# Position bias of an attention layer: coefficients in two fp16 parts under a scale found on the chip, and bias columns in another order

## The chip, the cores and the metric

The kernel runs on one core of a Trainium2 chip. The metric is the device time of one execution in microseconds (us). Five engines work side by side, each through its own instructions in a fixed order: PE (TensorE, matmuls; its weight loads are shown as PEld), DVE (VectorE), ACT (ScalarE), POOL (GpSimd) and SP (SyncE, which issues most DMAs). An instruction that waits holds up everything behind it on its engine, and nothing on the others unless they need its result.

## The reference

The program is an attention layer with a bias that depends on position, and behind it a gated feed-forward layer over all 2304 tokens:

```
q, k, v: (4, 8, 576, 64);  w1: (1, 32), b1: (32,), w2: (32, 8)
scores  = q @ k^T / sqrt(64)
x       = log1p(|i - j|) / log1p(max(i, 1))          # one number for each pair of positions
bias    = relu(x * w1 + b1) @ w2                     # (576, 576, 8), the same for all batches
attn    = softmax(scores + bias) ;  out = attn @ v
y       = (sigmoid(out @ w_gate) * (out @ w_val)) @ w_out
```

Inside the relu, each of the 32 hidden units is either off or a straight line in x. So for a given pair (i, j) the bias of head h is `A * x + B`, where A is the sum of `w2 * w1`, and B the sum of `w2 * b1`, over the units that are on. The kernel computes it so.

## The kernel before

`tile_kernel` first calls `bias`, then runs `attention` (units of one batch and two heads), then `Moe.run` (the feed-forward layer). The order of the instructions on every engine is written out in the Python code (`manual_schedule`), and so fixed.

**The bias stage.** The 576 columns j are worked off in nine chunks of 64 (`for c in range(NCH)`). For a chunk, 16 "indicator" tiles say which hidden unit is on: a tile has 4 columns j times 32 units on its partitions and all 576 rows i along it. Twelve of the 16 (`OWN`) are made by two matmuls into a PSUM tile `y` (L405) and a Sigmoid on ACT (L410); the first chunk makes some on DVE (L408). The other four (`DPAIRS`, tile `far`) are made by DVE from tables (`apart`, L423). The tiles of chunk c+1 are made while chunk c is summed: the lists `YPOS` and `DPOS` say behind which sums each is made.

The sums are matmuls with an indicator as stationary operand and the coefficients `cfs` as moving operand (`sums`, L429): 64 columns wide (A and B, 8 heads, 4 columns j). The coefficients `cf` are fp32. They are split into three bf16 parts (L472, L474), and each sum is three matmuls, one for each part. A chunk has five blocks of rows in the order `BORD` (blocks 0, 1, 4, 2, 3): four with 128 rows and 16 sums each, and block 4 with the last 64 rows and 8 sums. Every block has a PSUM tile `bps`, of which there are two. When its sums are done, `leave` takes it off: DVE multiplies the A half by x (`btmp`, L437, or L450 for block 4), and then the B half is added: by DVE straight from PSUM (L445, two instructions of 384 and 128 elements), or, for block 0 (`BPOOL`) and block 4, by ACT copying B into `brest` (L440) and POOL adding (L445, L455).

Beside this, in the order of each engine: `conv` lets DVE and ACT narrow weights for the feed-forward layer, a step behind each block (L227 on ACT, L230 to L239 on DVE), from 512 KB loads `cvw`; in chunks 3 to 6 a matrix of v is loaded as `vb` and multiplied with itself (`gram`, L352); in chunk 7 a power of two as scale for v is found (`fit`, L366 to L380). The last chunk makes no indicators. In front of the first chunk, 12 matmuls on zeros (L290) run while the small inputs arrive.

**The feed-forward stage.** `Moe.run` works through `ORDER` ("A0 A1 B0 A2 B1 A3 ..."): a step takes one of two token blocks (A, B) through one of 12 weight blocks. Each step has 12 matmuls into `pg`, 12 into `pu` (L999), and 9 into `po` for the step before (L1023). Weights are narrowed and split as they are needed: `convert` begins one new block and moves each block under way on by one step (size on ACT L227; clamp on DVE L230; bit operations on DVE L233, L236, L239; upper part on ACT L953; lower part on DVE L962). `pg` and `pu` have one buffer each. The three strings of `START` are done before the loop, in step 0 and in step 1; "s" issues a load, "w5" moves weight block 5 on by a step.

## Time and profile before

| | us |
|---|---|
| median of 3 runs (768.4 to 769.64) | 768.56 |
| the profiled execution, its own time | 767.42 |
| its span, first to last instruction | 765.6 |
| bias stage: first sum to first score matmul after the last chunk | 14.07 to 112.84 |
| feed-forward stage begins (first matmul of L999) | 343.9 |
| busy over the span: PE, DVE, ACT, POOL | 725.9, 625.8, 546.7, 335.4 |
| mean granted TensorE clock | 0.994 |

The profiled execution took 1.8 us more than its span, and 1.1 us less than the median. How to read what is shown below: a line of the timeline has start, duration, engine, source line, operation and operands, "x18" for so many instructions merged, and in brackets the idle time ahead of it with what ended it. A line of windows has a stretch, its length, the busy time (and number of instructions) of PE, PEld, DVE, ACT and POOL in it, the granted TensorE clock (1.00 is 2.4 GHz, 0.50 is 1.2 GHz), the busy share of the DMA engines and GB/s.

### The profile page before, as it was taken

To read this page: it belongs to the slowest core of one execution; us is meant where nothing else is said; L and a number is where in the kernel's file an instruction comes from. 1 tells how busy PE (TensorE), PEld (TensorE's weight loads), DVE (VectorE), ACT (ScalarE), POOL (GpSimd) and SP (SyncE) were. 2 spreads that over 40 slices of the span, in tenths; PEclk is the share of its full clock that TensorE was granted. 3 is DMA by queue.
4 is the path that set the end of the run, shared out by engine and by line. 5 is a ranking of instruction groups with operands and counts; after the bars stand their busy time and mean duration, and the time that the engine had idled before them with its cause. 6 is when DMAs were issued, how large, how long until landed. Compare 5 with 4: busy or idle time off the path is not lost.

```text
span 765.6 us, 17842 instructions
## 1 busy us (share of the span) xinstructions
PE 725.9 (95%) x6705; PEld 532.7 (70%) x6705; DVE 625.8 (82%) x1333; ACT 546.7 (71%) x1187; POOL 335.4 (44%) x430
## 2 busy tenths in 40 slices
PE   7998978999999998989999999989999999999997
PEld 4888866777777776768998999845555555555553
...
GB/s 208 134 200 190 148 61 113 176 177 192 152 203 166 172 216 216 174 199 323 190 251 249 183 100 96 128 192 151 81 83 83 56 56 131 145 48 64 56 1 82
DMA packets 128598, 111.85 MB, mean 146 GB/s; under 512 B 78848, under 2 KB 99456, under 8 KB 128512
## 3 DMA queue, kind: packets, MB, share of 16 engines
...
## 4 chain that ended last, share of the span: by engine, by line
PE 62%; DVE 9%; ACT 8%; DMA 3%; issue 3%; ACTq 0%; SPq 0%; POOL 0%; DVEq 0%
PE po L1023 17%; PE pg L1171 11%; PE pu L1171 8%; PE pg L999 6%; PE pu L999 6%; PE acc L743 5%; PE sc L635 4%; DVE en L651 4%; PE pt L680 3%; ACT at L565 3%; DVE at L566 3%; ACT en L656 2%; PE sc L624 1%; DMA vr<-in_v_dram 1%; DMA wo<-scratch 1%
## 5 line engine op out<-in xcount | busy, mean ns | idle before, releaser
L1129 POOL TENSOR_TENSOR ws<-wm 128x256 f32<-128x256 f32 x44 | 40.7, 924 | 284.9 <-ACT wv L1135 143.4
L1171 PEld LDWEIGHTS <-wv 128*128 128x128 f16 x1008 | 98.0, 98 | 84.0 <-issue 9.0
L656 ACT ACTIVATE en<-en,mn 128x576 f32<-128x576 f32 x144 | 110.7, 773 | 16.9 <-DVE mn L651 16.7
L1171 PE MATMUL pg<-xq,wv 128*128 128x384 f16 x576 | 109.3, 326 | 2.6 <-ACT c L1197 2.2
L651 DVE CUSTOM_DVE_ANT_0 en<-sc,bias 128x576 f32<-128x576 f32 x128 | 91.7, 754 | 10.1 <-PE sc L635 9.3
L674 POOL TENSOR_TENSOR cr<-en,cr 128x512 f16<-128x512 f32 x124 | 89.4, 742 | 5.2
L1023 PE MATMUL po<-wo,gh 128*128 128x512 f16 x288 | 85.7, 379 | 0.0
L1171 PE MATMUL pu<-xq,wv 128*128 128x384 f16 x432 | 82.0, 326 | 1.9 <-DVE c L1177 1.9
L635 PE MATMUL sc<-k,part 64*128 64x288 f32 x768 | 75.0, 314 | 3.5 <-DVE bias L445 1.8
L566 DVE SCALAR_TENSOR_TENSOR at<-pt,at 128x512 f16<-128x512 f32 (+3 forms) x132 | 72.0, 565 | 7.3 <-ACT at L565 5.8
L1177 DVE TENSOR_TENSOR c<-pu,c 128x384 f32<-128x384 f32 x72 | 39.9, 555 | 43.5 <-PE pu L1171 28.5
L635 PEld LDWEIGHTS sc<-k,part 64*128 64x128 f32 x768 | 58.7, 187 | 19.0 <-issue 10.8
L429 PE MATMUL bps<-cfs,ind 128*128 128x64 bf16 x1458 | 67.5, 193 | 3.5 <-DVE bias L445 1.7
L410 ACT ACTIVATE ind<-y 128x576 bf16<-128x576 f32 x100 | 62.4, 651 | 10.8 <-PE y L405 8.0
L743 PE MATMUL acc<-at,vv 128*64 128x288 f16 x868 | 65.8, 289 | 3.1 <-ACT xe L747 1.1
L565 ACT ACTIVATE at<-pt 128x512 f16<-128x512 f32 (+3 forms) x132 | 61.6, 493 | 8.9 <-PE pt L680 7.6
L429 PEld LDWEIGHTS <-ind 128*128 128x128 bf16 x1458 | 58.7, 98 | 9.7 <-issue 3.1
L1189 ACT ACTIVATE gh<-c 128x384 f16<-128x384 f32 x48 | 25.1, 522 | 54.7 <-DVE c L1187 53.3
L680 PE MATMUL pt<-ident,en 128*128 128x128 f32 x328 | 53.0, 285 | 7.8 <-ACT en L656 5.1
L743 PEld LDWEIGHTS <-vv 128*64 128x64 f16 x896 | 48.1, 109 | 17.7 <-issue 15.1
L1023 PE MATMUL po<-wo,gl 128*128 128x512 f16 x144 | 54.6, 379 | 0.0
L999 PE MATMUL pg<-xhi,w 128*128 128x384 f32 x192 | 53.8, 339 | 0.2
...
## 6 DMA issues: line engine op xcount, KB each, us to landing
...
```

The costliest lines, as they stand in the source:

```text
L429: nc.tensor.matmul(out=o, lhsT=st, rhs=cfs[:, part], start=(part == 0), stop=(part == 2))
L565: nc.scalar.activation(out=hi, in_=ps, func=AF.Copy, scale=float(2.0 ** up))
L566: return lambda: nc.vector.scalar_tensor_tensor(out=lo, in0=ps, scalar=float(2.0 ** up), in1=hi, op0=ALU.mult, op1=ALU.subtract)
L635: nc.tensor.matmul(out=pair[h][:, e, 0:HF], lhsT=qs[rows, l, 128 * it:128 * it + 128], rhs=ks[rows, r, HF * e:HF * e + HF], start=(i == 0) ...
L651: nc.vector.tensor_tensor_reduce(out=half(en), in0=ps[:, :, 0:HF], in1=half(nbias), scale=-0.125, scalar=3.0e38, op0=ALU.add, op1=ALU.min, ...
L656: nc.scalar.activation(out=en, in_=en, func=AF.Exp, bias=mn, scale=-1.0, accum_out=sm)
L674: nc.gpsimd.tensor_tensor(out=t[:, a:a + z.stop - z.start], in0=en[:, z], in1=t[:, z], op=ALU.subtract)
L680: nc.tensor.transpose(pt[:, J], en[:, 128 * J:128 * J + 128], ident)
L743: nc.tensor.matmul(out=acc[D * h:D * h + D, 0:HF], lhsT=vv[:, h, J, z], rhs=at[:, h, y, cs], start=(i == 0), stop=(i == len(mms) - 1))
L999: self.nc.tensor.matmul(out=(pg, pu)[z], lhsT=l, rhs=r, start=(kc == 0 and i == 0), stop=(kc == 3 and i == 2))
L1023: self.nc.tensor.matmul(out=po, lhsT=l[:, tt], rhs=r, start=(first and i == 0), stop=(last and i == 2))
L1171: nc.tensor.matmul(out=p, lhsT=W[i][:, l, at + kc], rhs=V[b][:, r, kc], start=(new and n == 0), stop=(n == 5), skip_group_check=not new)
```

## The change

1. The coefficients are split into two fp16 parts instead of three bf16 parts, and `sums` issues two matmuls instead of three. For this they are multiplied by a power of two `cup`, and the result is multiplied by `cun`. Both are found on the chip: ACT sums the squares of `cf`, POOL rounds the sum, a matmul with ones adds it over the partitions, and six small DVE instructions (`scales`) make the two powers of two.
2. The A half is unscaled by multiplying the table `xt` by `cun` once (five POOL instructions). The B half is unscaled where it is added: DVE's addition becomes a `scalar_tensor_tensor` with `cun` as a per-partition scalar, and ACT's copy takes `cun` as its scale.
3. The bias columns are stored in another order (first the first 32 columns of every chunk, then the second 32), so that the written pieces of a head are one run. The keys and values are put into the same order on the host.
4. In `START`, "w5 w5" moves from step 0 to step 1.

```diff
-START = 'w2 w3 w3 w2 w4 s w4 s', 's s s s w5 w5', ''
+START = 'w2 w3 w3 w2 w4 s w4 s', 's s s s', 'w5 w5'
...
+    order = np.arange(S).reshape(NCH, 2, 32).transpose(1, 0, 2).reshape(S)
+    data["k"], data["v"] = np.ascontiguousarray(data["k"][..., order]), data["v"][:, :, order]
...
-        biasL = keep.tile([128, NP, S], F32, name="biasL")
+        biasL = keep.tile([128, NP, 2, HF], F32, name="biasL")
...
+        nc.scalar.activation(out=room, in_=cf.rearrange("p a h g -> p (a h g)"), func=AF.Square, accum_out=total)
+        nc.gpsimd.tensor_copy(out=cmost, in_=total)
+        nc.tensor.matmul(out=ps[:, 0, 0:1], lhsT=ones, rhs=cmost, start=True, stop=True)
...
+            m, up, un = (t.bitcast(I32) for t in (total, cup, cun))
+            e = nc.vector
+            e.tensor_scalar(out=total, in0=ps[:, 0, 0:1], scalar1=float(2.0 ** -80), scalar2=None, op0=ALU.max)
+            e.tensor_scalar(out=m, in0=m, scalar1=1, scalar2=None, op0=ALU.logical_shift_right)
+            e.tensor_scalar(out=up, in0=m, scalar1=0x1FC00000 - (11 << 23), scalar2=None, op0=ALU.add)
+            e.tensor_scalar(out=un, in0=m, scalar1=0x1FC00000 - (12 << 23), scalar2=None, op0=ALU.add)
+            e.tensor_scalar(out=up, in0=up, scalar1=0x7F800000, scalar2=0x7F800000, op0=ALU.bitwise_and, op1=ALU.bitwise_xor)
+            e.tensor_scalar(out=un, in0=un, scalar1=0x7F800000, scalar2=None, op0=ALU.bitwise_and)
+        scales()
+        for n in range(5):
+            w = S if n < 4 else S - 32
+            nc.gpsimd.tensor_scalar(out=xt[:, n, 0:w], in0=xt[:, n, 0:w], scalar1=cun, scalar2=1.0, op0=ALU.mult, op1=ALU.mult)
...
-            for part in range(3):
-                nc.tensor.matmul(out=o, lhsT=st, rhs=cfs[:, part], start=(part == 0), stop=(part == 2))
+            for part in range(2):
+                nc.tensor.matmul(out=o, lhsT=st, rhs=cfs[:, part], start=(part == 0), stop=(part == 1))
...
-                nc.scalar.activation(out=rest, in_=ps[:, 0:n, 1], func=AF.Copy)
+                nc.scalar.activation(out=rest, in_=ps[:, 0:n, 1], func=AF.Copy, scale=cun)
...
-                rest, add = ps[:, 0:n, 1], nc.vector
+                rest = ps[:, 0:n, 1]
+                def put(out, in0, in1):
+                    nc.vector.scalar_tensor_tensor(out=out, in0=in0, scalar=cun, in1=in1, op0=ALU.mult, op1=ALU.add)
...
-                if not sub:
-                    nc.vector.tensor_copy(out=cfs[:, part], in_=cf)
-                elif part < 2:
-                    nc.vector.tensor_tensor(out=cf, in0=cf, in1=cfs[:, part], op=ALU.subtract)
+            if i == CFI:
+                nc.vector.tensor_scalar(out=cfs[:, 0], in0=cf, scalar1=cup, scalar2=None, op0=ALU.mult)
+                nc.vector.scalar_tensor_tensor(out=cfs[:, 1], in0=cf, scalar=cup, in1=cfs[:, 0], op0=ALU.mult, op1=ALU.subtract)
```

Three places show what moves. The first is DVE in front of the first chunk, before the change; `dist` and `edge` are the tables for `far`, and `ind` the indicators that DVE makes itself:

```order
L331 TENSOR_SCALAR dist<-dist,et 128x1152
L472 CAST cfs<-cf 128x64
L423 TENSOR_TENSOR far<-dist,edge 128x2x512
L474 TENSOR_TENSOR cf<-cf,cfs 128x64
L472 CAST cfs<-cf 128x64
L423 TENSOR_TENSOR far<-dist,edge 128x2x512
L474 TENSOR_TENSOR cf<-cf,cfs 128x64
L408 TENSOR_SCALAR ind_192<-y 128x576
```

And the same place of DVE after the change:

```order
L333 TENSOR_SCALAR dist<-dist,et 128x1152
L355 TENSOR_SCALAR ctotal<-bps 128x1
L356 TENSOR_SCALAR ctotal<-ctotal 128x1
L357 TENSOR_SCALAR cup<-ctotal 128x1
L358 TENSOR_SCALAR cun<-ctotal 128x1
L359 TENSOR_SCALAR cup<-cup 128x1
L360 TENSOR_SCALAR cun<-cun 128x1
L498 TENSOR_SCALAR cfs<-cf,cup 128x64
L499 SCALAR_TENSOR_TENSOR cfs<-cf,cup,cfs 128x64
L449 TENSOR_TENSOR far<-dist,edge 128x2x512 x2
L434 TENSOR_SCALAR ind_211<-y 128x576
```

Four small instructions that split `cf` have gone from between `far` and `ind`, and eight stand in front of `far`.

The second place is ACT in steps 0 and 1 of the feed-forward stage, before (`g` and `gh` are a step's gate; `w_1_7619` is the upper part of weight block 5, `w_0_...` and `w_2_...` those of other blocks):

```order
L1010 ACTIVATE gh<-g 128x384
L930 DMA ww<-scratch 128x512
L933 DMA ww<-in_moe_w_gate_dram 128x4x256
L933 DMA ww<-in_moe_w_val_dram 128x4x256
L933 DMA ww<-in_moe_w_out_dram 128x1024
L953 ACTIVATE w_1_7619<-ww 128x512
L972 ACTIVATE room,squares<-w_0_6677 128x512
L972 ACTIVATE room,squares<-w_0_6917 128x512
L953 ACTIVATE w_2_7665<-ww 128x512
```

And after, where `w_1_7030` is that upper part:

```order
L1035 ACTIVATE gh<-g 128x384
L955 DMA ww<-scratch 128x512
L958 DMA ww<-in_moe_w_gate_dram 128x4x256
L958 DMA ww<-in_moe_w_val_dram 128x4x256
L958 DMA ww<-in_moe_w_out_dram 128x1024
L997 ACTIVATE room,squares<-w_0_6045 128x512
L997 ACTIVATE room,squares<-w_0_6285 128x512
L978 ACTIVATE w_1_7030<-ww 128x512
L1033 ACTIVATE g<-pg 128x384
```

Block 5 now stands behind the two squares, and no further block is begun before the next gate.

The third place is DVE around the gate of step 4 (B1), before (`w_3_7798` and `w_3_7855` are the lower parts of the two weight blocks that step 5, A3, needs; `wm` is a block under way):

```order
L1009 TENSOR_TENSOR g<-pu,g 128x384
L962 TENSOR_TENSOR w_3_7798<-wm,w_3_7798 128x512
L233 TENSOR_SCALAR wm<-wm 128x512
L236 SCALAR_TENSOR_TENSOR wm<-ww,wm 128x512
L239 SCALAR_TENSOR_TENSOR wm<-ww,wm 128x512
L230 TENSOR_SCALAR wm<-wm 128x512
L962 TENSOR_TENSOR w_3_7855<-wm,w_3_7855 128x512
```

And after, where the two are `w_3_7212` and `w_3_7225`:

```order
L1034 TENSOR_TENSOR g<-pu,g 128x384
L235 TENSOR_SCALAR wm<-wm 128x512
L238 SCALAR_TENSOR_TENSOR wm<-ww,wm 128x512
L241 SCALAR_TENSOR_TENSOR wm<-ww,wm 128x512
L232 TENSOR_SCALAR wm<-wm 128x512
L987 TENSOR_TENSOR w_3_7212<-wm,w_3_7212 128x512
L235 TENSOR_SCALAR wm<-wm 128x512
L238 SCALAR_TENSOR_TENSOR wm<-ww,wm 128x512
L241 SCALAR_TENSOR_TENSOR wm<-ww,wm 128x512
L232 TENSOR_SCALAR wm<-wm 128x512
L1036 TENSOR_TENSOR gl<-g,gh 128x384
L987 TENSOR_TENSOR w_3_7225<-wm,w_3_7225 128x512
```

Between the gate of step 4 and each of the two lower parts stands one more set of four bit operations, and `gl` too has moved ahead of the second. From the gate of step 5 on, the two orders are the same.

## Rows read from the trace of the kernel before

**Rows 1.** Windows: chunk 1, and the sum over chunks 1 to 7.
```profile
20.80:31.60 10.80, 10.33 (x259) 9.41 (x256) 7.32 (x17) 9.67 (x17) 3.22 (x6) 1.00 0.55 180
...
sum 77.30, PE 72.17 PEld 66.33 DVE 63.62 ACT 62.88 POOL 30.50; mean PE 10.31 PEld 9.48 DVE 9.09 ACT 8.98 POOL 4.36
```

**Rows 2.** Groups of instructions of the page: the sums on the `ind` tiles.
```profile
L429 PE MATMUL bps<-cfs,ind 128*128 128x64 bf16 x1458 | 67.5, 193 | 3.5 <-DVE bias L445 1.7
```

**Rows 3.** Timeline of PE, at the first sums and inside chunk 3.
```profile
14.07 0.69 PE L429 MATMUL bps<-cfs,ind 128*128 128x64 bf16 x18 [0.39 <-ACT ind L410]
14.59 0.34 PE L429 MATMUL bps<-cfs,far 128*128 128x64 bf16 x6
...
46.00 0.41 PE L405 MATMUL y<-lt,wy 128*128 128x288 bf16 x2
46.25 0.51 PE L429 MATMUL bps<-cfs,ind 128*128 128x64 bf16 x12
```

**Rows 4.** Waits of the bias stage: us in total, times, longest.
```profile
DVE btmp L437 <- PE bps L429: 7.4, 10, 1.7
...
DVE btmp L450 <- ACT brest L440: 6.5, 5, 2.5
...
ACT cvm L227 <- DMA cvw<-in_moe_w_out_dram: 0.7, 1, 0.7
```

**Rows 5.** Lines L1070, L1009, L1034: duration in ns, min/median/max.
```profile
L1070 DVE SCALAR_TENSOR_TENSOR xq<-xt,ups,xq x28: 604/611/1100, 477.9 to 620.9; 128x384 f16<-128x384 f32 x28
...
L1009 DVE TENSOR_TENSOR g<-pu,g x24: 548/556/558, 348.5 to 493.3; 128x384 f32<-128x384 f32 x24
...
L1034 ACT ACTIVATE ob<-po,uns x8: 677/687/687, 639.4 to 761.3; 128x512 f32<-128x512 f32 x8
L1034 ACT ACTIVATE ob<-po x4: 576/583/592, 482.0 to 502.5; 128x512 f32<-128x512 f32 x4
```

**Rows 6.** Timeline of PE and DVE ahead of chunk 0, and of DVE in `fit`.
```profile
8.40 0.66 PE L405 MATMUL y<-lt,wy 128*128 128x288 bf16 x4 [1.79 <-DVE wy L325]
...
9.68 0.19 DVE L472 CAST cfs<-cf 128x64 bf16<-128x64 f32 x1
...
11.50 0.75 DVE L408 TENSOR_SCALAR ind<-y 128x576 bf16<-128x576 f32 x1
...
98.45 0.15 DVE L374 TENSOR_SCALAR vnorm<-bps 128x1 f32<-128x1 f32 x1
...
99.25 0.33 DVE L380 TENSOR_TENSOR vout<-vun,small 128x1 f32<-128x1 f32 x1
```

**Rows 7.** Line L239 in `conv` (ns, min/median/max), and POOL's timeline beside the longest.
```profile
L239 DVE SCALAR_TENSOR_TENSOR cvm<-cvw,cvm x9: 677/680/1676, 36.4 to 107.1; 128x512 int32<-128x512 int32 x9
...
106.84 1.40 POOL L570 TENSOR_TENSOR k<-kr,k 128x576 fp32r<-128x576 f32 x1
```

**Rows 8.** Feed-forward stage: timelines of PE and DVE, and the chain that ended last.
```profile
354.10 0.50 PE L1023 MATMUL po<-w,gl 128*128 128x512 f32 x1 [0.67 <-DVE gl L1011]
...
373.50 0.68 DVE L962 TENSOR_TENSOR w<-wm,w 128x512 fp32r<-128x512 f32 x1
374.10 0.42 DVE L233 TENSOR_SCALAR wm<-wm 128x512 int32<-128x512 int32 x1
...
376.23 0.68 DVE L962 TENSOR_TENSOR w<-wm,w 128x512 fp32r<-128x512 f32 x1
...
375.02 2.10 PE pg L999 x12
377.12 2.08 PE pu L999 x12
```

**Rows 9.** Windows around the end of the bias stage.
```profile
104.00:108.00 4.00, 2.74 (x89) 2.50 (x86) 3.93 (x8) 0.38 (x1) 1.83 (x2) 1.00 0.27 78
112.00:114.00 2.00, 1.02 (x11) 0.82 (x11) 0.88 (x3) 0.00 (x0) 0.00 (x0) 1.00 0.03 8
116.00:118.00 2.00, 2.00 (x13) 1.39 (x10) 1.24 (x3) 1.56 (x4) 0.29 (x1) 0.50 0.00 0
```

More of the change, by code (lines that the diff above doesn't have):

```diff
@@ L187, in tile_kernel @@
         over = pool("over", first, "right")
-        biasL = keep.tile([128, NP, S], F32, name="biasL")
+        biasL = keep.tile([128, NP, 2, HF], F32, name="biasL")
         ident = keep.tile([128, 128], F32, name="ident")
         make_identity(nc, ident)
-        biases = over.tile([128, 24, S], F32, name="bias0"), keep.tile([128, 8, S], F32, name="bias3")
+        biases = over.tile([128, 2, 24, HF], F32, name="bias0"), keep.tile([128, 2, 8, HF], F32, name="bias3")
         def extra(n):
@@ L212, in tile_kernel @@
         else:
-            nc.sync.dma_start(out=out[0:512, 0:512].rearrange("(c p) j -> p c j", p=128), in_=biases[1][:, 4:8, 0:512])
+            nc.sync.dma_start(out=out[0:512, 0:512].rearrange("(c p) j -> p c j", p=128), in_=ident.to_broadcast([128, 4, 512]))
 def narrow(nc, t, lo, hi, eng, sized=None):
@@ L337, in bias, with scales @@
             nc.gpsimd.tensor_scalar(out=cf[:, ab], in0=cf[:, ab], scalar1=wb[:, ab:ab + 1], scalar2=8.0, op0=ALU.mult, op1=ALU.mult)
+        ones = cp.tile([128, 128], BF16, name="ones")
+        nc.gpsimd.memset(ones, 1.0)
+        total, cup, cun = (cp.tile([128, 1], F32, name=n) for n in ("ctotal", "cup", "cun"))
+        cmost = cp.tile([128, 1], BF16, name="cmost")
+        room = cp.tile([128, 2 * H * 4], F32, name="croom")
+        nc.scalar.activation(out=room, in_=cf.rearrange("p a h g -> p (a h g)"), func=AF.Square, accum_out=total)
+        nc.gpsimd.tensor_copy(out=cmost, in_=total)
+        nc.tensor.matmul(out=ps[:, 0, 0:1], lhsT=ones, rhs=cmost, start=True, stop=True)
+        def scales():
+            m, up, un = (t.bitcast(I32) for t in (total, cup, cun))
[10 more added lines that the diff above has]
+            nc.gpsimd.tensor_scalar(out=xt[:, n, 0:w], in0=xt[:, n, 0:w], scalar1=cun, scalar2=1.0, op0=ALU.mult, op1=ALU.mult)
         conv = moe.narrow_ahead(pool("cvw", 2), pool("cvm", 2))
         vp = pool("vb", 2)
[L340 removed]
         squares = cp.tile([128, B], F32, name="vsq")
@@ L452, in leave @@
                 r = slice(64 * s_, 64 * s_ + 64)
-                j = slice(64 * c + 32 * s_, 64 * c + 32 * s_ + 32)
                 for e in range(2):
-                    add.tensor_tensor(
-                        out=biasL[64 * e:64 * e + 64, :, j], in0=rest[r, 0, e::2], in1=tmp[r, 0, e::2], op=ALU.add)
+                    put(biasL[64 * e:64 * e + 64, :, s_, 32 * c:32 * c + 32], rest[r, 0, e::2], tmp[r, 0, e::2])
         def load_vb(b):
@@ L463, in bias @@
         ind, own, far = switches(0, lt)
-        cfs = cp.tile([128, 3, 2, H, 4], BF16, name="cfs")
+        cfs = cp.tile([128, 2, 2, H, 4], F16, name="cfs")
         for i, f in enumerate(own):
@@ L468, in bias @@
                 far.pop(0)()
-            part, sub = divmod(i - CFI, 2)
-            if part in range(3):
-                if not sub:
-                    nc.vector.tensor_copy(out=cfs[:, part], in_=cf)
-                elif part < 2:
-                    nc.vector.tensor_tensor(out=cf, in0=cf, in1=cfs[:, part], op=ALU.subtract)
+            if i == CFI:
+                nc.vector.tensor_scalar(out=cfs[:, 0], in0=cf, scalar1=cup, scalar2=None, op0=ALU.mult)
+                nc.vector.scalar_tensor_tensor(out=cfs[:, 1], in0=cf, scalar=cup, in1=cfs[:, 0], op0=ALU.mult, op1=ALU.subtract)
         lt = load_lx(1)
@@ L651, in run @@
             nc.vector.tensor_tensor_reduce(
-                out=half(en), in0=ps[:, :, 0:HF], in1=half(nbias), scale=-0.125, scalar=3.0e38,
+                out=half(en), in0=ps[:, :, 0:HF], in1=nbias, scale=-0.125, scalar=3.0e38,
                 op0=ALU.add, op1=ALU.min, accum_out=mn)
```

12 lines of the change are left out of this document (5 added, 7 removed).

## The prediction

> **What bounds the kernel now.** The change is in the bias stage, before the first score matmul, and at the start of the feed-forward stage, so I read those two alone, first by windows, then by waits, then line by line.
>
> Chunk 1 to chunk 7 together take 77.3 us, in which PE is busy for 72.2, DVE for 63.6 and ACT for 62.9 [rows 1]. PE is the bound, but by no great margin: the two others are at 81 to 82%. Inside a chunk PE runs sum after sum. 18 of them start within 0.52 us, so one costs 28.9 ns; a pair of y matmuls costs 0.25 us [rows 3]. A chunk has 72 sums, so 216 matmuls, 6.2 us, and 12 pairs of y, 3.0 us. DVE's idle time has two main causes: it waits 7.4 us for the sums, and 6.5 us ahead of L450 for ACT's copy of block 4 [rows 4]. The last chunk is different: between 104 and 108 us DVE is busy for 3.93 of 4 us and PE for 2.74 [rows 9], so DVE is the bound there already.
>
> At the start of the feed-forward stage PE has only one wait, 0.67 us for `gl` at 354.10, and from there to 378 it runs without a gap: pg of step 5 at 375.02, pu at 377.12 [rows 8].
>
> **The change, part by part.** The sum is made against the profiled execution, 767.42 us.
>
> *Removed: a third of the sums.* 648 of 1944 matmuls go, of which the page shows 1458 on `ind` alone [rows 2]. At 28.9 ns they are 18.7 us of PE: 14.6 in chunks 1 to 7 (504 matmuls), 2.1 in each of chunks 0 and 8. This is not the gain, since DVE and ACT must follow.
>
> *Added to each chunk.* Three additions per chunk, of two instructions each, become `scalar_tensor_tensor` with a scalar read per partition. The nearest row has that form over 384 elements, 611 ns; a plain addition of 384 takes 556 [rows 5]. I take 55 ns more for each: 42 instructions in chunks 1 to 7 make 2.3 us of DVE. The bounds are 0 and, with twice the price, 4.6. ACT's copy with a scale per partition took 687 ns against 583 [rows 5], so 0.1 us for each of two copies a chunk. POOL's additions keep their form.
>
> *Chunks 1 to 7.* PE falls to some 58 us, and DVE becomes the bound with 63.6 + 2.3 = 65.9. In chunk 1, where `conv` gives DVE nothing yet, ACT is busier: 9.67 + 0.2 against 7.32 + 0.33 [rows 1], which adds 2.2, so 68.1. I leave 0.4 of idle time, 68.5 in all: **-8.8 us**. The bounds: if DVE alone counted, -11.4; if only DVE's wait for the sums went and the one ahead of L450 stayed, -7.4 + 2.3 = -5.1 [rows 4]; with loads that come late, -3 (a rival below). I choose the value near the upper end because PE will be ahead by most of a block, and the copy that L450 waits for stands behind block 4's sums, so this wait should shrink too.
>
> *Chunk 0.* By its first block-4 multiply it has done 40 sums, so 1.2 us less; I take **-0.9** (0 to -1.2), since the first chunk's DVE work is partly behind the sums.
>
> *Chunk 8.* No gain, since DVE is the bound, and eight dearer additions: **+0.4** (0 to 0.5).
>
> *The start.* Six small DVE instructions find the scale. The same six in `fit` took 99.25 - 98.45 = 0.80 us [rows 6]. Two instructions for `cfs` stand behind them, some 0.4 us by the durations of the split before, and four go that lay between 9.68 and 11.50, about 0.6 us of those 1.82 [rows 6]. DVE comes to its first indicator some 0.6 us later, and PE's last y matmuls wait for the buffers that DVE frees. The wait in PE's queue for the scale's matmul costs nothing by itself: behind it stand the y matmuls, which wait for `wy` until 8.40 anyway, idle for 1.79 [rows 6]; ACT's square and POOL's rounding come right behind `cf`, well before that. Without that cover it would delay all y matmuls. But the second y pair into `bps` now needs the buffer that holds the scale's sum, and so DVE's read at about 9.7, 0.5 us later than now; it is the same delay, not a second one. The five scalings of `xt` on POOL (each at most the 1.40 us of L570 [rows 7]) start when `cun` is there, at about 10.5; the first is needed only when block 0's sums, which begin at 14.07 [rows 3], are done, and the others a block later each, so that they are hidden. But DVE's four instructions on `cfs` and `far` meet them. One L239 took 1676 ns where 680 is usual, beside an addition of 1.40 us on POOL [rows 7]: 1.0 us lost. I take one such loss of 0.6, together **+1.2**; with none, +0.5; with four of 1.0, +4.6.
>
> The Trainium skill (SBUF — State Buffer, SBUF: two separate sides) speaks against the change here: DVE and GpSimd share a pair of ports, and an instruction that needs them is blocked until the other's ends. The trace agrees with it in L239's row. By that rule each of the four could lose a whole POOL instruction, and the sum would come out at -3.3 and not -6.7; not all of the trace's DVE instructions beside POOL are longer, so I keep the smaller loss.
>
> *The order of weight block 5.* Its upper and lower part leave the way of `gl` of step 0, so PE's wait of 0.67 goes [rows 8]. But one block fewer is begun by step 4, and the lower parts that step 5 needs come later. Before, DVE does the first at 373.50 and the second at 376.23, with one set of four bit operations between (374.10 to 376.23, 2.13 us) [rows 8]. Now a set stands ahead of the first, which starts at 375.63 and ends at 376.31. Pg of step 5 needs it in its third matmul, 0.35 us behind 375.02: PE waits 0.94. Then lower part (0.60), set (2.13) and `gl` (0.56, as in [rows 5]) put the second at 378.92, done at 379.60, while pu, now at 378.06, needs it at 378.41: 1.19 more. Both starts move with PE by the same 0.67, so the whole is 0.94 + 1.19 - 0.67 = **+1.4**, and PE, full from there on, doesn't win it back. The bounds: -0.7 if the parts come in time, and 378.92 - 376.23 = +2.7 if the wait at `gl` only moves.
>
> *Nothing:* the other order of the bias columns (as many instructions and elements, and the softmax reads as many).
>
> **The sum:** 1.2 - 0.9 - 8.8 + 0.4 + 1.4 = -6.7, so 760.7 for the profiled execution. The median stands 1.1 above it, which gives 761.9; I say 762.
>
> **The rivals.**
> *More of it (15 in 100).* DVE runs without idle time, the start loses nothing to POOL, and step 5 doesn't wait: 0.6 - 1.2 - 11.4 + 0.4 - 0.7 = -12.3, so 756.3. For it: DVE runs so in chunk 8 [rows 9]. Against it: ACT has only some 0.5 us a chunk to spare then, and each y needs an answer from it.
> *The loads come late (17 in 100).* ACT's step on a new `cvw` waited 0.7 us for its load already [rows 4]. A load has some four of a chunk's five steps to land; a chunk that is 1.25 us shorter takes 1.0 of it. Five or six loads that each hold ACT for 1.0, and by the indicators PE, give back 5.5: -1.2, so 767.4.
> *Slower: the clock falls (7 in 100).* In the first half of the stretch 112 to 118 PE was busy for about half of the time, and then it ran at 0.50 [rows 9], that is 1.2 GHz. With 7.2 us of PE work in a chunk of 9.3 to 9.8, PE is busy for about three quarters. At half the clock these become 14.3 us, 4.5 to 5 a chunk more; one and a half such chunks eat up the 6.7, and three give 776. Against it: PE at 2.74 of 4 us kept 1.00 [rows 9].
> *The two parts cost what three did (5 in 100).* No row has an fp16 operand against a bf16 one. At 43 ns a matmul the first two terms fall away, and 1.2 + 0.4 + 1.4 and DVE's 2.3, as far as it shows, give 772 to 774.
>
> **How the numbers follow.** The forecast, 758.5 to 765.5, gets 56 in 100; its range takes up the bounds of the start (+2), of step 5 (-2.1, +1.3) and 2 us on chunks 1 to 7. The range 756 to 768 leaves out the two slower cases (12) and the far end of the first (4). 0.2% is 1.5 us, about what a measurement can tell from no change. Faster: 56 + 15 + half of the loads' 17, so 0.80; same: the other half, 0.08; slower: 0.12.
>
> **What would show it.** Right: chunks of 9.2 to 10 us with DVE at 95% or more and PE near 80%; bias additions of 610 ns over 384 elements; the first sums at about 15.2; DVE as busy in chunk 8 as now; no wait at `gl` of step 0, and two waits of about 1 us at step 5 for L987. Wrong: waits of ACT for `cvw`, a granted clock below 1.00 inside the bias stage, sums of more than 29 ns, or a start later than 16 us.

## The result: slower by 0.8%

The changed kernel takes 774.29 us (median of 8 runs, 771.89 to 776.28), the kernel before 767.73 on the same chip (8 runs, 766.65 to 770.26). The ratio is 1.0077, with a 95% interval of 1.0056 to 1.0099. Predicted were 762 us, with a range from 756 to 768. The profiled execution took 772.53 us, its span is 770.7 (765.6 before), its mean granted clock 0.987 (0.994).

PE has a third fewer matmuls in its sums, at the same price for each, and no chunk became much shorter. The windows (columns as in [rows 1]) are those of chunk 1, of chunk 5, and the sum over chunks 1 to 7. A chunk is counted throughout from the start of DVE's multiply of block 4 (L480, formerly L450) to the next one.

```profile
22.30:32.50 10.20, 8.82 (x184) 7.59 (x182) 7.74 (x17) 9.21 (x17) 3.23 (x6) 1.00 0.54 189
...
64.60:78.00 13.40, 10.54 (x189) 9.21 (x188) 9.57 (x21) 8.98 (x16) 4.31 (x7) 0.87 0.88 221
...
sum 78.30, PE 62.97 PEld 54.16 DVE 65.89 ACT 62.46 POOL 30.39; mean PE 9.00 PEld 7.74 DVE 9.41 ACT 8.92 POOL 4.34
```

DVE is busy for 2.3 us more than in [rows 1], as predicted, and PE for 9.2 less (14.6 were forecast; part of the difference is chunk 5, where PE works at a low clock, and the rest is not taken apart here). Yet the seven chunks take 78.3 us and not 77.3. No engine fills them now: DVE is busy for 84% of them. The page's group of the sums answers to [rows 2]:

```profile
L455 PE MATMUL bps<-cfs,ind 128*128 128x64 f16 x972 | 52.6, 194 | 14.1 <-DVE bias L474 7.8
```

The idle time ahead of these sums rose from 3.5 to 14.1 us. The waits between 14 and 112 us (us in total, times, longest) say for what, first as they were before the change, as far as [rows 4] doesn't show them, and then after it:

```profile
ACT brest L440 <- DVE btmp L437: 5.8, 7, 2.4
...
PE y L405 <- ACT ind L410: 3.9, 10, 1.5
...
PE bps L429 <- DVE bias L445: 1.7, 3, 1.1
...
PE bps L429 <- ACT brest L440: 0.7, 2, 0.5
```

```profile
ACT brest L466 <- DVE btmp L463: 10.3, 8, 2.6
...
DVE btmp L480 <- ACT brest L466: 8.7, 6, 3.7
...
PE bps L455 <- DVE bias L474: 7.8, 16, 1.5
PE y L431 <- ACT ind L436: 6.7, 12, 1.5
PE bps L455 <- ACT brest L466: 5.6, 7, 1.0
...
DVE btmp L463 <- PE bps L455: 4.1, 5, 1.8
```

Only the last of them shrank, DVE's wait for the sums (7.4 in [rows 4]). ACT's wait for DVE's multiply of block 0 grew from 5.8 to 10.3, DVE's wait for ACT's copy of block 4 from 6.5 to 8.7, and PE's waits for DVE's additions and ACT's copies from 1.7 and 0.7 to 7.8 and 5.6. The timeline of DVE, ACT and PE in chunk 3, sorted by time, shows how these waits hang together:

```profile
42.94 0.42 DVE L480 TENSOR_TENSOR btmp<-bps,xt 128x256 f32<-128x256 f32 x1 [0.56 <-issue]
...
48.14 0.68 DVE L449 TENSOR_TENSOR far<-dist,edge 128x1024 bf16<-128x1024 f16 x1
48.74 0.68 DVE L463 TENSOR_TENSOR btmp<-bps,xt 128x512 f32<-128x512 f32 x1
49.54 0.69 ACT L466 ACTIVATE brest<-bps,cun 128x512 f32<-128x512 f32 x1 [1.11 <-DVE btmp L463]
50.28 0.28 PE L455 MATMUL bps<-cfs,ind 128*128 128x64 f16 x4 [0.75 <-ACT brest L466]
50.82 0.41 PE L431 MATMUL y<-lt,wy 128*128 128x288 bf16 x2 [0.26 <-ACT ind L436]
...
51.66 1.28 PE L379 MATMUL bps<-vb 128*128 128x128 bf16 x20
...
53.06 0.47 ACT L466 ACTIVATE brest<-bps,cun 128x256 f32<-128x256 f32 x1 [0.55 <-PE bps L379]
...
53.64 0.42 DVE L480 TENSOR_TENSOR btmp<-bps,xt 128x256 f32<-128x256 f32 x1 [0.96 <-ACT brest L466]
```

It is a ring. From block 4's multiply to block 0's of the next chunk (48.74) DVE works in its order, almost without a gap. ACT's copy of block 0 waits for that multiply. Block 4's sums need the `bps` buffer of block 0, there being two, and so wait for the copy. Behind them stand y, `gram`, ACT's copy of block 4, and DVE's next multiply, 10.70 us after the last one. Of a chunk's 72 sums only the 8 of block 4 lie on this ring.

Where the profiled executions differ, by the start of the same instruction in both: the first block-4 multiply comes 1.5 us later; chunks 1 to 4 are 0.4 shorter and chunks 5 to 7 1.4 longer; from there to the first score matmul 0.2 is lost, from that to the first output of the attention 1.6 (26.3 against 24.7), up to the first L1024 0.4, and behind it 0.4. That is the 5.1 us between the spans. The medians lie 6.6 apart; the profiled execution of the changed kernel is 1.8 below its median. (The first score matmul starts at 110.67 before the change and at 113.43 after it; the 112.84 of the table of times is the second one, behind a wait.)

In chunk 5, and from the last sums of chunk 8 on, the granted clock is low, at the second place for longer than in [rows 9]. Windows of both places:

```profile
72.00:74.00 2.00, 0.49 (x8) 0.34 (x8) 1.96 (x5) 1.53 (x3) 1.97 (x3) 1.00 0.43 156
74.00:76.00 2.00, 2.00 (x26) 1.82 (x24) 0.33 (x2) 1.47 (x3) 0.42 (x1) 0.52 0.91 264
...
112.00:114.00 2.00, 2.00 (x30) 1.62 (x27) 1.39 (x4) 0.00 (x0) 1.46 (x4) 0.50 0.77 248
...
118.00:120.00 2.00, 1.93 (x12) 1.58 (x12) 0.62 (x3) 1.99 (x4) 0.00 (x0) 0.50 0.03 8
```

PE's timeline has `gram` of chunk 5, whose 20 matmuls took 1.28 us in chunk 3:

```profile
74.99 2.34 PE L379 MATMUL bps<-vb 128*128 128x128 bf16 x20
```

The start, as DVE's and PE's timelines show it, answers to [rows 6] and [rows 3]:

```profile
4.09 0.15 DVE L300 TENSOR_SCALAR et<-small 128x1 f32<-128x1 f32 x1 [4.09 <-DMA small<-in_small_dram]
...
11.38 0.65 DVE L499 SCALAR_TENSOR_TENSOR cfs<-cf,cup,cfs 128x64 f16<-128x64 f32 x1
11.95 1.77 DVE L449 TENSOR_TENSOR far<-dist,edge 128x1024 bf16<-128x1024 f16 x2
13.65 0.74 DVE L434 TENSOR_SCALAR ind<-y 128x576 bf16<-128x576 f32 x1
...
15.55 0.51 PE L455 MATMUL bps<-cfs,ind 128*128 128x64 f16 x12
```

DVE's first indicator comes 2.15 us later than in [rows 6]. 0.66 of that is no part of the change: `small` landed at 4.09, against 3.43 in the profile of before and 3.15 to 3.69 in all the runs below. Step 5 of the feed-forward stage, PE's timeline:

```profile
379.87 0.62 PE L1024 MATMUL pg<-xhi,w 128*128 128x384 f32 x2 [1.00 <-DVE w L987]
...
383.07 0.62 PE L1024 MATMUL pu<-xhi,w 128*128 128x384 f32 x2 [0.84 <-DVE w L987]
```

### The profile page after: what moved, and what is told of

Same layout as the page of the kernel before. It is cut to its first block, busy times and chain, and to the rows that moved or that the text cites. A ratio compares the mean times of both kernels' runs of the same rounds, so it can differ in the third digit from the quotient of the medians.

```text
span 770.7 us, 16565 instructions
## 1 busy us (share of the span) xinstructions
PE 716.0 (93%) x6058; PEld 519.8 (67%) x6058; DVE 630.3 (82%) x1336; ACT 547.2 (71%) x1189; POOL 343.2 (45%) x436
## 4 chain that ended last, share of the span: by engine, by line
PE 60%; DVE 9%; ACT 8%; DMA 3%; issue 3%; POOL 1%; SPq 0%; ACTq 0%; DVEq 0%; POOLq 0%
PE po L1048 16%; PE pg L1196 10%; PE pu L1196 7%; PE pg L1024 6%; PE pu L1024 6%; PE acc L768 5%; PE sc L660 4%; PE pt L705 3%; DVE en L676 3%; ACT at L590 3%; ACT en L681 2%; DVE at L591 2%; PE sc L649 1%; DMA vr<-in_v_dram 1%; DMA wo<-scratch 1%
## 5 line engine op out<-in xcount | busy, mean ns | idle before, releaser
L1154 POOL TENSOR_TENSOR ws<-wm 128x256 f32<-128x256 f32 x44 | 43.1, 979 | 283.6 <-DMA xt<-xs 145.1
L660 PE MATMUL sc<-k,part 64*128 64x288 f32 x768 | 77.3, 319 | 2.8 <-DVE bias L474 1.4
L1202 DVE TENSOR_TENSOR c<-pu,c 128x384 f32<-128x384 f32 x72 | 39.9, 554 | 42.7 <-PE pu L1196 28.0
L660 PEld LDWEIGHTS sc<-k,part 64*128 64x128 f32 x768 | 60.5, 191 | 19.0 <-issue 13.1
L455 PE MATMUL bps<-cfs,ind 128*128 128x64 f16 x972 | 52.6, 194 | 14.1 <-DVE bias L474 7.8
L436 ACT ACTIVATE ind<-y 128x576 bf16<-128x576 f32 x100 | 60.5, 650 | 6.4 <-PE y L431 5.8
L1214 ACT ACTIVATE gh<-c 128x384 f16<-128x384 f32 x48 | 25.1, 522 | 54.0 <-DVE c L1212 52.5
L455 PEld LDWEIGHTS <-ind 128*128 128x128 bf16 x972 | 45.4, 99 | 23.1 <-issue 10.8
L1024 PE MATMUL pg<-xhi,w 128*128 128x384 f32 x192 | 53.9, 339 | 1.2 <-DVE w L987 1.0
```

Of the source, the lines that this page charges most:

```text
L455: nc.tensor.matmul(out=o, lhsT=st, rhs=cfs[:, part], start=(part == 0), stop=(part == 1))
L660: nc.tensor.matmul(out=pair[h][:, e, 0:HF], lhsT=qs[rows, l, 128 * it:128 * it + 128], rhs=ks[rows, r, HF * e:HF * e + HF], start=(i == 0) ...
L1024: self.nc.tensor.matmul(out=(pg, pu)[z], lhsT=l, rhs=r, start=(kc == 0 and i == 0), stop=(kc == 3 and i == 2))
```

## The experiments

Theory A: the ring sets the chunk, and with PE's sums gone its waits grow instead. Theory B: the saving was there, and the dearer additions took it. Each kernel was timed against the kernel before on the same chip; the table has the median, the ratio to before with its interval, and from the profiled execution the length of chunks 1 to 4 and 5 to 7 and the time from the first score matmul to the attention's first output (us).

| kernel | median | ratio to before | chunks 1-4 | chunks 5-7 | to first output |
|---|---|---|---|---|---|
| before | 767.73 | 1 | 42.7 | 34.6 | 24.7 |
| changed | 774.29 | 1.0077 [1.0056, 1.0099] | 42.3 | 36.0 | 26.3 |
| e6_two_bf16 | 767.92 | 0.9999 [0.9988, 1.0010] | 40.7 | 37.0 | 24.7 |
| e1_third_zero | 775.48 | 1.0092 [1.0075, 1.0109] | 44.2 | 34.8 | 25.2 |
| e2_plain | 772.68 | 1.0060 [1.0041, 1.0079] | 40.7 | 36.7 | 25.7 |
| e4_far_late | 771.85 | 1.0039 [1.0023, 1.0055] | 41.2 | 33.8 | 25.2 |
| e9_before_far_late | 768.31 | 1.0000 [0.9989, 1.0011] | 42.8 | 34.4 | 25.3 |
| e5_copy_first | 775.73 | 1.0107 [1.0078, 1.0136] | 43.1 | 34.7 | 25.4 |
| e18_clock | 772.29 | 1.0056 [1.0038, 1.0074] | 42.3 | 34.4 | 25.6 |
| e10_scale_late | 772.56 | 1.0062 [1.0046, 1.0077] | 42.3 | 35.9 | 26.2 |
| e20_order | 770.20 | 1.0024 [1.0011, 1.0037] | 42.7 | 34.1 | 25.8 |
| e3_start | 771.15 | 1.0050 [1.0031, 1.0070] | 42.3 | 35.8 | 26.5 |
| e19_layout | 767.03 | 1.0001 [0.9984, 1.0017] | 42.7 | 34.6 | 25.3 |
| e12_far_start_load | 770.73 | 1.0044 [1.0027, 1.0061] | 41.1 | 34.3 | 26.2 |
| e13_load_early | 776.06 | 1.0108 [1.0085, 1.0130] | 42.3 | 37.3 | 25.7 |
| e14_all | 772.92 | 1.0060 [1.0040, 1.0080] | 41.1 | 37.4 | 25.4 |
| e15_all_clock | 770.61 | 1.0037 [1.0023, 1.0051] | 41.1 | 36.1 | 25.1 |
| e16_three | 770.10 | 1.0030 [1.0013, 1.0047] | 41.1 | 34.3 | 24.9 |
| e17_three_clock | 771.12 | 1.0043 [1.0028, 1.0058] | 41.1 | 33.8 | 25.3 |

Chunks 1 to 4 repeat within 0.02 us among the five kernels that leave them as changed, and within 0.08 among the six with `far` late, so differences of a few tenths there are real. The whole is less certain: the versions were timed on several chips, and where the intervals of their ratios overlap, a difference of their medians alone shows little.

### Where the saving went

**e6_two_bf16**, on the kernel before:

```diff
-            for part in range(3):
-                nc.tensor.matmul(out=o, lhsT=st, rhs=cfs[:, part], start=(part == 0), stop=(part == 2))
+            for part in range(2):
+                nc.tensor.matmul(out=o, lhsT=st, rhs=cfs[:, part], start=(part == 0), stop=(part == 1))
```

> The kernel before with two matmuls in every sum instead of three, and nothing else changed (the lowest of the three bf16 parts is left out of the sum): the saving of PE alone, without scale, dearer additions, POOL's work and the order of weight block 5. Theory A (the ring): chunks 1 to 7 lose at most 2 us of 77.3, and PE's thin work lets the clock fall, so the whole stays within 765.5 to 769.5 (before 767.7). Theory B (dearer additions took the gain): the forecast's gain shows, chunks 1 to 7 at 67 to 69 us, the whole at 757 to 760.

The saving of PE alone, with nothing added, is worth nothing: ratio 0.9999. Windows of its chunk 1, chunk 5, and the sum of chunks 1 to 7:

```profile
20.15:30.05 9.90, 8.72 (x181) 7.48 (x178) 7.43 (x18) 9.12 (x17) 3.23 (x6) 1.00 0.59 191
...
60.85:74.65 13.80, 10.46 (x190) 9.33 (x188) 9.57 (x22) 8.81 (x16) 4.26 (x7) 0.88 0.99 230
...
sum 77.75, PE 64.00 PEld 55.37 DVE 64.23 ACT 61.51 POOL 31.09; mean PE 9.14 PEld 7.91 DVE 9.18 ACT 8.79 POOL 4.44
```

Chunks 1 to 4 win 2.0 us, a quarter of the 8.3 that 288 matmuls fewer take; chunks 5 to 7, where the clock falls as in the changed kernel, lose 2.4. Theory B falls with this run: it needs a gain of some 8 us that the additions take away, and without them there are 2.0 in chunks 1 to 4 and none in the whole.

**e1_third_zero**, on the changed kernel:

```diff
-            for part in range(2):
+            for part in range(3):
...
+        nc.gpsimd.memset(cfs[:, 2], 0.0)
```

> The changed kernel with a third matmul in every sum, on a part that is all zero: the output is the same, PE works as much as before the change. Theory A (the chunk is set by a ring of waits in program order, in which only block 4's sums lie: DVE from block 4's multiply to block 0's of the next chunk, ACT's copy of block 0, PE's sums of block 4, ACT's copy of block 4, DVE again): chunks 1 to 7 stay between 76.5 and 79.5 us (78.3 in the changed kernel), the clock in chunk 5 and behind chunk 8 falls less, and the whole comes to 770 to 775 (changed kernel 774.3). Theory B (fewer matmuls did save the forecast 8.8 us, and the dearer additions and the clock took it away again): 8 us more, 780 to 784.

A third matmul in all 648 sums costs 1.2 us by the medians (the two intervals overlap), and not 8; the median is just above the 770 to 775 of theory A. Chunks 1 to 4 get 1.9 us longer, so PE fills them again; chunks 5 to 7 get 1.2 shorter, since the clock stays at 1.00 there.

**e2_plain**, on the changed kernel:

```diff
-                nc.scalar.activation(out=rest, in_=ps[:, 0:n, 1], func=AF.Copy, scale=cun)
+                nc.scalar.activation(out=rest, in_=ps[:, 0:n, 1], func=AF.Copy)
...
-                    nc.vector.scalar_tensor_tensor(out=out, in0=in0, scalar=cun, in1=in1, op0=ALU.mult, op1=ALU.add)
+                    nc.vector.tensor_tensor(out=out, in0=in0, in1=in1, op=ALU.add)
```

> The changed kernel with plain additions of the B half on DVE and plain copies on ACT, as before the change (the B half is left unscaled, everything else as changed). Theory A: two of the three pairs of additions and both copies lie on the ring, 0.12 and some 0.1 us each, so chunks 1 to 4 get about 0.4 us shorter each (9.9, 9.9, 10.4 and 10.6 us, as in the kernel before with two bf16 parts, against 10.2, 10.4, 10.7 and 11.0), and the whole comes to 771.5 to 773.5 (774.3). Theory B (the dearer additions ate the forecast's gain): chunks of 9.2 to 9.6 us, the whole at 766 to 768.

As theory A had it: 1.6 us less by the medians (the two intervals overlap), and chunks of 9.93, 9.87, 10.38 and 10.55 us, those of e6_two_bf16 within 0.06. So the scalar per partition costs 0.39 us a chunk, two pairs of additions and two copies on the ring, and fp16 operands cost what bf16 ones do. It costs as much where PE has all its work: chunks 1 to 4 take 44.2 us in e1_third_zero and 42.7 before the change, with three matmuls in both. So PE was not the only thing that set a chunk, even before.

### The ring

**e4_far_late** on the changed kernel, **e9_before_far_late** on the kernel before, the same edit (17 puts the first `far` behind block 0's multiply):

```diff
-DPOS = [20, 36, 52], [6, 22, 38]
+DPOS = [20, 36, 52], [17, 22, 38]
```

> The changed kernel with one of DVE's table indicators (far, 0.6 us) issued behind block 0's multiply instead of ahead of it, the same work in another place. Theory A (the ring): 0.6 us less in each chunk in which the ring closes without a gap, chunks 1 to 7 at 74 to 76 us (78.3), the whole at 769.5 to 772 (774.3). Theory B (the amount of DVE work with its dearer additions sets the chunk): no change, 773.5 to 775.

> The kernel before with one of DVE's table indicators (far) issued behind block 0's multiply, nothing else. Theory A (before the change PE and the ring were nearly equally long, PE at 10.3 of 11.0 us a chunk): a shorter ring gains little where PE fills the chunk, 0 to 0.3 us a chunk, 766 to 768 (before 768). Rival (far's place helps by itself, whatever PE does): the 3.3 us that chunks 1 to 7 gained from it in the changed kernel, 764 to 765.

The same 0.6 us of DVE work in another place gives the changed kernel 2.4 us by the medians (the intervals of the ratios don't overlap), and chunks 1 to 7 fall from 78.3 to 75.0; 1.7 of these 3.3 us are chunk 5, where the clock now stays at 1.00. The kernel before gets nothing from it (1.0000). That is what a ring and an engine of nearly equal length do: before, PE was about as long, so a shorter ring alone (e9) gives nothing, and fewer sums alone (e6) give a quarter of their time in chunks 1 to 4 and nothing in the whole; with both (e4), chunks 1 to 7 are 2.3 us shorter than before. In chunks 1 to 4 the gain is 0.3 a chunk, not the expected 0.6, and PE of e4_far_late shows why, in chunk 3:

```profile
45.27 0.41 PE L455 MATMUL bps<-cfs,ind 128*128 128x64 f16 x8 [0.28 <-DVE bias L474]
47.38 0.51 PE L455 MATMUL bps<-cfs,ind 128*128 128x64 f16 x12 [0.26 <-DVE bias L474]
49.11 0.28 PE L455 MATMUL bps<-cfs,ind 128*128 128x64 f16 x4 [0.15 <-ACT brest L466]
```

The wait for the copy of block 0 fell from 0.75 to 0.15; those for DVE's additions, which free the buffers of blocks 2 and 3, stayed. They are a second strand.

**e5_copy_first**, on the changed kernel; ACT's copy stands ahead of DVE's multiply in `leave`:

```diff
-            if blk < 4:
-                x = xt[:, blk, js].rearrange("p (s o j) -> p s o j", s=2, o=1)
-                nc.vector.tensor_tensor(out=tmp, in0=ps[:, :, 0], in1=x.to_broadcast([128, 2, H, 32]), op=ALU.mult)
             if blk in BPOOL and c < NCH - 1 or blk == 4:
...
+            if blk < 4:
+                x = xt[:, blk, js].rearrange("p (s o j) -> p s o j", s=2, o=1)
+                nc.vector.tensor_tensor(out=tmp, in0=ps[:, :, 0], in1=x.to_broadcast([128, 2, H, 32]), op=ALU.mult)
```

> The changed kernel with ACT's copy of block 0 ahead of DVE's multiply of block 0 (as block 4 has it), so that the copy does not wait for DVE. Theory A (the ring): PE gets the buffer for block 4 some 0.4 us earlier, 0.2 to 0.5 us less a chunk, the whole at 770.5 to 773 (774.3); the wait of ACT's copy for DVE's multiply, 7.7 us in the changed kernel, goes. Theory B (DVE's work): no change, 773.5 to 775.

A miss. ACT's wait for the multiply went, but its waits (20 to 112 us) show PE behind the additions for 13.5 us (7.8), and chunks 1 to 4 are 0.8 longer:

```profile
PE bps L455 <- DVE bias L470: 13.5, 20, 2.1
...
DVE btmp L474 <- ACT brest L462: 2.2, 5, 1.1
```

Multiply and copy read one `bps` tile, and whichever is second waits: the wait changes hands. The Trainium skill (PSUM — Partial Sum Buffer, PSUM bank collisions raise a hardware error) says that two engines must not touch one bank of a partition quadrant (32 partitions) at a time, reads included, and that the compiler adds a dependency between such instructions. The traces agree with the order (1.11 us of ACT ahead of 49.54); no run here let the two overlap.

### The granted clock

**e18_clock**, on the changed kernel, with e1's zero part in chunk 5 and the last chunk alone:

```diff
-                        sums(ps[:, i // 8, :, :, 4 * (i % 8):4 * (i % 8) + 4], ind[i % 8][:, i // 8, o:o + 128])
+                        sums(ps[:, i // 8, :, :, 4 * (i % 8):4 * (i % 8) + 4], ind[i % 8][:, i // 8, o:o + 128], 3 if c in (5, NCH - 1) else 2)
```

> The changed kernel with a third matmul on a zero part in each sum of chunk 5 and of the last chunk, nothing else. If PE's thinner work lets the clock fall there, and the fallen clock costs what the traces show (chunk 5 13.4 us against 12.0 with three parts; the first attention unit 26.3 against 25.2): chunk 5 at 12 to 12.5 us, 2 to 2.5 us less in all, 771.5 to 772.5 (774.3). Rival (the ring alone sets these stretches): chunk 5 above 13, 774 to 775.

More work for PE, 2.0 us less by the medians (the two intervals overlap). Chunk 5 falls from 13.42 to 11.80 us. Its window, and the same `gram`:

```profile
74.00:76.00 2.00, 2.00 (x40) 1.92 (x39) 0.60 (x3) 1.56 (x3) 0.81 (x2) 1.00 0.59 187
...
74.71 1.28 PE L379 MATMUL bps<-vb 128*128 128x128 bf16 x20
```

PE still waits 1.39 us for ACT there (1.51 in the changed kernel). Up to the end of that wait chunk 5 takes nearly as long in both, 9.11 us in the changed kernel and 8.98 here. Windows of the rest of it, up to the next multiply of block 4, of the changed kernel and then of e18_clock:

```profile
73.72:78.03 4.31, 4.31 (x50) 3.94 (x50) 0.61 (x4) 2.33 (x5) 0.70 (x1) 0.60 0.89 192
...
73.87:76.69 2.82, 2.82 (x55) 2.64 (x55) 0.73 (x4) 2.27 (x5) 0.94 (x2) 1.00 0.70 204
```

PE is busy throughout in both, and 1.5 of the 1.6 us lie here. So what went is the low clock, which held `gram` and the sums around it.

### The start, the order of block 5, and the column order

**e10_scale_late**, on the changed kernel:

```diff
+        def unscale():
+            nc.gpsimd.tensor_copy(out=cmost, in_=ind[DPAIRS[1]][:, 0, 0:1])
+            for n in BORD:
...
+            if i == 4:
+                unscale()
```

> The changed kernel with POOL's five scalings of the table xt held back until DVE has written its second far (a one-element POOL copy of it stands ahead), and in the order in which the blocks use them. If it is POOL that makes DVE's split of cfs (0.65 us) and the two far (1.77 us in all) long: they fall to 0.3 and 1.3 us, the first indicator of DVE comes 0.7 to 0.9 us earlier, and the whole goes down by up to that, 773 to 774.3 (774.3). Rival (the two are long by their form): they stay, no change.

DVE's rows answer to 11.38 and 11.95 above:

```profile
10.62 0.28 DVE L504 SCALAR_TENSOR_TENSOR cfs<-cf,cup,cfs 128x64 f16<-128x64 f32 x1
10.82 1.28 DVE L452 TENSOR_TENSOR far<-dist,edge 128x1024 bf16<-128x1024 f16 x2
12.03 0.75 DVE L437 TENSOR_SCALAR ind<-y 128x576 bf16<-128x576 f32 x1
```

0.65 became 0.28, 1.77 became 1.28, so POOL beside DVE had cost 0.9 us. Counted from the landing of `small`, the first block-0 multiply comes 0.5 us earlier than in the changed kernel (12.47 against 13.00, and 12.24 before the change). The whole is 1.7 us less by the medians, more than that explains, but the two intervals overlap.

**e20_order**, part 4 of the change alone on the kernel before, and **e3_start**, the changed kernel without it:

```diff
-START = 'w2 w3 w3 w2 w4 s w4 s', 's s s s w5 w5', ''
+START = 'w2 w3 w3 w2 w4 s w4 s', 's s s s', 'w5 w5'
```

> The kernel before with the start order of the change alone (part 4: weight block 5 in step 1). Working of the prediction: PE's wait of 0.7 for gl goes and two waits of about 1 us for lower parts come in step 5, so 1.1 to 1.4 us more, 769 to 769.6 (before 768). Rival (won back later): 767.5 to 768.5.

> The changed kernel with weight block 5 back in step 0 (the start order of before), all else as changed. If the move costs what the trace of the changed kernel shows at step 5 (waits of 1.0 and 0.8 us for L987 against 0.7 for gl): 1.1 us less, 772.5 to 773.5 (774.3), with the wait of 0.7 for gl back and no wait of PE at step 5. Rival (the two waits are made up for later): no change, 774 to 775.

Alone, the order costs 0.24% (0.11 to 0.37), 1.8 us, with the two waits in PE's timeline:

```profile
377.28 0.63 PE L999 MATMUL pg<-xhi,w 128*128 128x384 f32 x2 [1.00 <-DVE w L962]
...
380.48 0.62 PE L999 MATMUL pu<-xhi,w 128*128 128x384 f32 x2 [0.83 <-DVE w L962]
```

e3_start has neither, and a wait for `gl` of 0.4. Its median is 3.1 us below the changed kernel, more than the order explains; its runs spread from 770.05 to 775.14, and the two intervals overlap.

**e19_layout**, part 3 alone on the kernel before (the diff's lines on `order`, `biasL`, `biases` and `nbias`, with plain additions):

```diff
-        biasL = keep.tile([128, NP, S], F32, name="biasL")
+        biasL = keep.tile([128, NP, 2, HF], F32, name="biasL")
```

> The kernel before with the other order of the bias columns alone (part 3 of the change, with keys and values in that order). The prediction counted it as nothing: 767.5 to 769 (before 768). Rival (the softmax reads the new layout more slowly, and that is what e16_three still loses): 770 to 771, with the lines of the softmax longer than before.

1.0001: the column order costs nothing.

### Put together

All on the changed kernel; e12 has `far` late, the old start order and

```diff
-CSTEPS = [2, 6, 10, 14, 18, 22, 26, 30, 34]
+CSTEPS = [2, 6, 10, 14, 18, 22, 27, 31, 35]
```

> The changed kernel with far late, the start order of before, and the last three narrowed weight blocks of the bias stage begun a block later each (so that ACT's step on the load issued in chunk 5 comes a block later). Theory A with the load as the second cause in chunk 5: e4_far_late's 771.9 less 1.1 for the start order and less 0.5 to 1 for chunk 5 (11.7 us to about 11), so 769.5 to 770.5, with no wait of ACT for cvw. Rival (the load's wait is hidden): 770.5 to 771.

The load was misread: the one that ACT waits for in chunk 5 is begun at step 22, and the edit moved later ones. ACT still waited 1.2 us for `cvw`. The median is 1.1 us below e4_far_late, what the old order should give, but the ratio is not below e4's (1.0044 and 1.0039), so this run doesn't show it. **e13_load_early** moves the right one, and **e14_all** puts this together with e4, e10 and e3:

```diff
-CSTEPS = [2, 6, 10, 14, 18, 22, 26, 30, 34]
+CSTEPS = [2, 6, 10, 14, 18, 21, 26, 30, 34]
```

> The changed kernel with one narrowed weight block begun one block earlier (step 21 instead of 22), so that its 512 KB load goes out ahead of the load vb and not 1.3 us behind it. If that load is what makes the hole of PE in chunk 5: ACT does not wait for cvw, the clock stays at 1.00 there, chunk 5 falls from 13.4 to 11.3 to 12 us, and the whole to 772 to 773 (774.3). Rival (the hole is the ring's and the clock's, the load comes late beside it): chunk 5 above 13, no change of the whole.

> The changed kernel with what the runs so far point to: far behind block 0's multiply, POOL's scalings held back until the second far is written, the start order of before, and the load of step 22 a block earlier. Theory A, summed from the runs: 771.9 with far late, less 1.1 (start order), less 0.7 (scalings), less 0.5 (load) gives 769.5; with a higher granted clock 768. Rival (the gains do not add up, since the clock falls the more, the thinner PE's work): 770.5 to 772.

Both miss. The load came in time, but begun a step earlier the block finds its `cvm` buffer still being written out, as the waits of e13_load_early between 60 and 90 us say; chunk 5 took 14.9 and 16.0 us:

```profile
ACT cvm L229 <- DMA scratch<-cvm: 4.6, 1, 4.6
```

**e15_all_clock**, **e16_three** and **e17_three_clock**: e15 is e14 with the zero part in the last chunk (`3 if c == NCH - 1 else 2`); e16 is e14, and e17 is e15, both with the old `CSTEPS`:

```diff
-CSTEPS = [2, 6, 10, 14, 18, 21, 26, 30, 34]
+CSTEPS = [2, 6, 10, 14, 18, 22, 26, 30, 34]
```

> The kernel of e14_all with a third matmul on a zero part in each sum of the last chunk alone, where PE waits for DVE anyway. If the clock that falls behind the bias stage costs what the first attention unit shows (26.3 us from the first score matmul to its first output, against 24.7 in the kernel before): 1 to 1.5 us less than e14_all. Rival (the clock falls there in any case, as in the kernel before between 115 and 119): within 0.5 us of e14_all.

> The changed kernel with far behind block 0's multiply, POOL's scalings held back behind the second far, and the start order of before (e14_all without the earlier load, which had made ACT wait 4.6 us for a buffer). If ring, start and order are causes that add up: 771.9 (e4_far_late) less 1.1 and less 0.7, so 770, and chunk 5 at 11.5 to 12 us. Rival (the clock takes the rest back): 771 to 772.5.

> The kernel of e16_three with a third matmul on a zero part in each sum of the last chunk alone. If the clock behind the bias stage is the fourth cause: 1 to 2 us less than e16_three, as e15_all_clock was 2.3 below e14_all, so 768 to 769, as fast as the kernel before. Rival: within 0.5 us of e16_three.

e15 is 2.3 us below e14, but 1.3 of that is chunk 5, which the edit leaves alone. e16 comes out as summed, 770.1, with chunk 5 at 12.3 and not 11.5 to 12. e17 doesn't: 771.1, with runs from 766.5 (granted clock 0.993) to 772.9 (0.979). So a clock that falls behind the last chunk is not shown as a cause of its own: e18_clock shows it for chunk 5. No version is faster than the kernel before.

## Why the prediction was wrong

**What bounds the kernel: right in part.** PE did fill the chunks before (e9_before_far_late gains nothing, e1_third_zero fills PE again). But close behind it stood a ring of waits, not DVE's busy time, and the ring had a share in the chunk even then: with PE's full work the dearer additions still add 1.5 us to chunks 1 to 4 (e1_third_zero against before).

**The step that failed is the term for chunks 1 to 7, -8.8.** It measured +1.0; without the 1.6 us that the low clock cost in chunk 5 it would be -0.6. It said "DVE becomes the bound", and took the value near the upper end "because PE will be ahead by most of a block, and the copy that L450 waits for stands behind block 4's sums, so this wait should shrink too". PE can't be ahead: block 4 needs the buffer of block 0, whose copy waits for DVE's multiply, and the wait at L450 grew by 2.2 us, 1.2 of them in chunk 5. Both readings were in [rows 4], where DVE's 6.5 us for the copy stand beside its 7.4 for the sums; they were taken for idle time that goes when PE is quicker, and ACT's wait of 5.8 us for DVE's multiply, in the same list of waits, was not looked at. All bounds, -3 to -11.4, had that in them; no gain at all was not among them. The saving of PE without any of the rest (e6_two_bf16) would by the same terms have been forecast at about -12 (63.6 of DVE, 2.4 for ACT in chunk 1 and 0.4 idle make 66.4 us for chunks 1 to 7; chunk 0 gives -0.9) and gave 0.

**The dearer additions: right in size, wrong in place.** A pair's spacing went from 0.67 (45.91 to 46.58 in chunk 3 of the trace of before) to 0.79 us (44.91 to 45.70), so 60 ns for each against 55 foretold. The durations (ns, min/median/max, both sizes together) reach 619, where 610 was said for the longer one:

```profile
L474 DVE SCALAR_TENSOR_TENSOR bias<-bps,cun,btmp x56: 340/480/619, 20.9 to 114.9; 128x384 f32<-128x384 f32 x28, 128x128 f32<-128x128 f32 x28
```

Two of a chunk's three pairs and the two copies lie on the ring, so e2_plain gives back the 0.39 a chunk in full.

**The start, +1.2: right mechanism, too small.** Without the late arrival of `small` DVE is 1.5 us later. The loss to POOL was taken as one of 0.6; e10_scale_late shows 0.9 (0.37 and 0.49). The rule of the Trainium skill that was weighed there (SBUF — State Buffer, SBUF: two separate sides) would have given up to 4.6; the trace shows DVE's instructions held up, not each for a whole POOL instruction (POOL's five take 4.68 us, so 0.94 each).

**Chunk 0 and chunk 8.** The block-4 multiply of chunk 0 is 0.85 later, by `small` corrected, where +0.3 was the sum of the first two terms; the saving by itself is 0.8 there (e6_two_bf16, corrected too), so that -0.9 was right and the start is what was missed. Chunk 8 took 10.55 against 10.61: nothing, where +0.4 was foretold. That it comes near is luck: with plain additions it takes 9.93 (e2_plain) or 9.54 (e6_two_bf16), so fewer sums do gain 0.7 or more there, where no gain was foretold, and the dearer additions take it back.

**Block 5: right.** The wait for `gl` went, and 1.00 and 0.84 came where 0.94 and 1.19 were foretold: +1.2 for +1.4, and e20_order shows 1.8 (0.8 to 2.8) in the whole. The column order costs nothing, as said.

**The rivals.** "Slower: the clock falls", held at 7 in 100, came in part, and not as it was priced. It was to come from chunks in which PE is busy for three quarters; chunks 1 to 4 keep 1.00 with PE busy for 80 to 86%. It came in chunk 5, behind the hole of 1.0 and 1.5 us that ring and load leave PE, and cost 1.6 us there (e18_clock); the 1.6 us at the attention's first unit go with a clock at 0.50 too, but e17_three_clock doesn't confirm them as its price. From the first score matmul to the first output the mean granted clock is 0.77 in the changed kernel's trace, 0.93, the highest of all traces, in that of before, and 0.86 or 0.87 in e9, e19 and e20, which have PE's work of before and take 25.3 to 25.8 us. The clock there differs from one execution to the next of the same code, and it isn't all (e6_two_bf16 takes 24.7 at 0.86). Against those three the changed kernel loses 0.5 to 1.0 us, so how much of the 1.6 is the change's stays open. "The loads come late" did not come: ACT's wait for `cvw` is 0.6 us (0.7). Nor did "the two parts cost what three did": with plain additions the fp16 sums take as long as the bf16 ones (e2_plain against e6_two_bf16).

**What stays open.** With ring, POOL and order mended, e16_three is still 0.3% slower, with a bias stage that ends 0.6 us later than before. In its profiled execution 2.6 us are lost between the attention's first output and the feed-forward stage (211.2 us against 208.6), where the changed kernel took 208.9 and others up to 211.4. The three kernels with the attention of before, e6, e9 and e20, take 209.8 to 210.4, so an execution can lose some 2 us there without the change; whether e16_three's loss is of that kind is not settled.
